# Weights in four pieces and some reordered steps in a recurrent-attention and squared-ReLU kernel

## The chip, the core and the metric

The kernel runs on one core of one Trainium2 chip. The metric is the time of one execution on the device in microseconds (us). The core has five engines that run side by side: PE (TensorE, the matmuls), DVE (VectorE), ACT (ScalarE), POOL (GpSimd) and SP (SyncE, which here only issues transfers). Each engine takes its instructions strictly in the order in which the program lists them; they meet only at semaphores.

## What is computed

The reference first runs a gated recurrence and then a two-layer block on its output:

```
for t in range(S):                                  # B, H, S, D = 4, 8, 768, 48
    state = alpha[:, :, t, :, None] * state + einsum('bhd,bhe->bhde', k[:, :, t], v[:, :, t])
    y[:, :, t] = einsum('bhd,bhde->bhe', q[:, :, t], state)
x = y.transpose(0, 2, 1, 3).reshape(3072, 384)
h = x @ w_in                                        # 384 -> 2048
out = (max(h, 0) ** 2) @ w_out                      # 2048 -> 384
```

Inputs and output are float32; the kernel multiplies in bf16.

## The kernel before, in words

**Units.** The 3072 tokens are cut into 12 units of 256 tokens, numbered 0 to 11 (four batches, three stretches each, all first stretches first). The first unit is unit 0, so the "second unit" of the change is unit 1 and the "third" is unit 2. A unit g passes these steps; the names are those of the kernel's tables, with the line that does the work and the engine:

- `lda`, `ldk`, `ldq`, `ldv` g (L463): load alpha, k, q, v, on SP's queue, or on POOL's for units 1 to 3.
- `pr` (L570, product of two neighbouring decays, DVE or POOL), `ln` (L573, ACT, its logarithm), `m1i` (L579 and L582, PE, running sums into the PSUM bank W), then three readers of that bank on ACT: `ei` (L590), `ea` (L592), `ec` (L595). For units 2 and 3 a second sum `m1s` (L579) goes into the same bank and is read by `es` (L604). For units from 4 on, `lm` (L612, ACT) and `lb` (L614, DVE) take its place.
- `bk`, `aq` (L597 to L608), `eqm0`, `eqm1` (L641), `ekm` (L646): products with decays, all from SBUF to SBUF, on DVE (`bk2` on POOL).
- `tr0`, `tr1` (L669 on PE with copies `et0`, `et1` for units 1 and 2; L657 as transfers on SP from unit 3 on).
- `p` (L877 and L730): scores and state products on PE; `mk0`, `mk1` (L894, DVE) apply the mask; `sa`, `sc`, `sd` carry the state.
- `y` (L757, L765, PE): the unit's output; `xe`, `xf` (L911, L913) copy it out; `xt` (L929, PE, for units 1 to 3) transposes it; `xv` (L941) copies that into the operand of the first layer.
- `s1_g_u`, u from 0 to 7 (L992, PE): a group of six matmuls, the first layer for 256 of the 2048 hidden columns. `re` g_u (L1000 on ACT, L1002 on DVE) is max(h, 0) out of PSUM, `sq` (L1010, L1013, L1014) the square.
- `s2_g_j_s` (L1038, PE): four matmuls each, the second layer; `oe` copies its result out, `out` stores it.

**The order.** Five tables (L206 to L268), one for each engine, write down every instruction's place by name. PE follows its table without overtaking. `+512` and `+256` are matmuls on zeros (L1086) that fill PE's first 17 us.

**The hidden groups' banks.** The first 16 first-layer groups, in the order unit 0 then unit 1, use the PSUM banks that this string names, and all later groups alternate between 0 and 1:

```
HIDDEN = "0102102102102101"
```

The digit 2 is bank O, 0 and 1 are the two H banks. A group that comes into a bank must wait until the `re` of the group that held it before has read it. So group s1_0_5 (the sixth digit) and group s1_1_0 (the ninth) both use H bank 0, s1_0_7 and s1_1_2 use H bank 1, and s1_2_0 and s1_2_2 use H bank 0.

**The weights.** `w_in` and `w_out` are loaded on POOL's queue and converted to bf16 on the way (`weight`, L426 to L436). `PIECES` (L317) says how 16 blocks of 128 hidden columns are cut into transfers: 8, 4 and 4 of them. Inside a piece the columns are dealt out with a stride that is the piece's number of blocks (`hidden`, L417). Group s1_g_u needs blocks 2u and 2u+1, so it waits for one piece. `AFTER` (L1063) holds back transfers until an earlier one has landed: unit 2's alpha (`lda2`) until unit 1's v, each piece of `w_out` likewise, unit 4's alpha until unit 3's.

Of the kernel before, what the change touches and what calls it, by code (L numbers as in the profile page):

```python
# [26 lines left out]
class Program:  # L27
# [12 lines left out]
    def add(self, eng, fn, cost, prio, reads=(), writes=(), name="", dma=None, lag=0, after=(), mode=("F", "F"),  # L40
            alts=None):

        reads, writes = ([h for k in keys for h in ((k + (0,), k + (1,)) if len(k) == self.HALVED.get(k[0]) else (k,))]
                         for keys in (reads, writes))
        choices = {eng: (fn, cost)}
        if alts:
            choices.update(alts)
        op = Op(choices, prio, name)
        op.idx = len(self.ops)
        op.lag = lag  # L50
        op.mode = mode
        if dma is not None:
            if dma not in self.dma_sems:
                self.dma_sems[dma] = self.nc.alloc_semaphore("d_" + dma)
                self.dma_count[dma] = 0
            self.dma_count[dma] += 1
            op.sem = (dma, self.dma_count[dma])
        for o in after:
            op.deps[o] = True
        for k in reads:  # L60
            w = self.writer.get(k)
            if w is not None:
                op.deps[w] = True
            if k[0] == "ps":
                for r in self.readers.get(k, ()):
                    if r not in op.deps:
                        op.deps[r] = False
                        op.shared.add(r)
        for k in writes:
            w = self.writer.get(k)  # L70
            if w is not None:
                op.deps[w] = True
            for r in self.readers.get(k, ()):
                if r is not op:
                    op.deps.setdefault(r, False)
                    op.shared.discard(r)
        for k in reads:
            self.readers.setdefault(k, []).append(op)
        for k in writes:
            self.writer[k] = op  # L80
            self.readers[k] = []
        op.deps.pop(op, None)
        self.ops.append(op)
        return op
# [88 lines left out]
    def emit(self):  # L173
# [33 lines left out]
    "act": """  # L207
        table ln0_0 ln1_0 ei0_0 xcaus ea0_0 ei1_0 ea1_0 ec1_0 et00_0 ec0_0 vc0 ln1 et01_0 et11_0 vc1 ei1 ea1 xe0
        ec1 xv0 sa1 re0_0 re0_1 sq0_1 re0_3 xe1 re0_4 re0_5 ln2 re0_6 sq0_6 ei2 ea2 ec2 vc2 re1_2 es2 re1_3
        re1_4 et0_2 sq1_3 re1_6 sa2 sq1_6 oe0_0 ln3 ei3 ea3 ec3 oe0_1 es3 xf2 xe2 lm4 ln4 vc3 ei4 ea4 ec4 re2_0  # L210
        re2_1 es4 oe1_0 re2_2 re2_3 re2_4 ldk5 re2_5 ldq5 sa3 sq2_5 lm5 re2_7 ln5 re2_6 xe3 ei5 ea5 ec5 xv3 es5
        oe2_0 re3_0 oe2_1 lm6 re3_1 xe4 ln6 re3_4 re3_3 ei6 ea6 ec6 re3_6 sq3_5 re3_7 sq3_7 es6 re4_0 re4_1
        re4_2 re4_3 vc6 xe5 lm7 ln7 re4_7 oe3_1 re4_4 ei7 ea7 ec7 re4_6 sq4_6 es7 oe4_0 re5_0 re5_1 lm8 ln8 xe6
# [7 lines left out]
    "dve": """  # L221
        zero zlinc zlstr zident zcaus zcaus1 zla0 zla1 zones zown zown0 zown1 zqk0 zqk1 zqk2 zlb0 zlb1 ekm0_0
        eqm0_0 ekm1_0 eqm1_0 et10_0 mk0_0 sa0 mk1_0 ekm1 eqm0_1 eqm1_1 et0_1 et1_1 sc0 mk1_1 mk0_1 sc1 re0_2 xf1
        sq0_3 pr2 xv1 sq0_5 re0_7 re1_0 re1_1 ekm2 sq0_7 aq2 eqm0_2 eqm1_2 re1_5 et1_2 sq1_1 sq1_5 re1_7 mk1_2
        pr3 sq1_7 sc2 mk0_2 bk3 eqm1_3 ekm3 aq3 eqm0_3 pr4 xv2 bk4 lb4 ekm4 eqm1_4 eqm0_4 sq2_1 mk1_3 mk0_3 sc3
        oe1_1 sd3 sq2_7 sq2_6 xf3 lb5 ekm5 eqm1_5 eqm0_5 sa4 mk1_4 mk0_4 re3_2 pr6 sc4 sq3_1 xf4 sq3_3 re3_5
        sq3_6 lb6 ekm6 sa5 mk0_5 sc5 mk1_5 eqm0_6 eqm1_6 oe3_0 xf5 sq4_1 re4_5 pr7 sq4_3 sq4_7 sq4_5 bk7 lb7
        eqm0_7 sa6 eqm1_7 ekm7 sc6 sd6 mk0_6 mk1_6 pr8 oe4_1 xf6 sq5_3 bk8 lb8 ekm8 sq5_5 sq5_6 sa7 mk0_7 sc7
# [6 lines left out]
    "pe": """  # L235
        +512 +512 +512 +512 +512 +512 +512 +512 m10_0 m11_0 +512 +512 +256 +256 tr00_0 +512 +256 tr10_0 +512
        +256 +256 tr01_0 p0_0 tr11_0 kv0 +512 +512 +512 +256 +256 p1_0 m11 +512 +256 y0 +512 +512 +256 tr0_1 xt0
        tr1_1 +512 +512 +512 +256 p0_1 s1_0_0 s1_0_1 s1_0_3 s1_0_2 y1 s1_0_4 s1_0_5 xt1 s1_0_6 s1_0_7 m1i2
        s1_1_0 s1_1_1 s1_1_2 m1s2 s1_1_3 s1_1_4 tr0_2 s1_1_6 s1_1_5 tr1_2 s2_0_0_0 s1_1_7 p0_2 s2_0_0_1 s2_0_0_2
        s2_0_0_3 s2_0_1_0 s2_0_1_1 m1i3 s2_0_1_2 s2_0_1_3 m1s3 y2 s2_1_0_0 s2_1_0_1 xt2 s2_1_0_2 m1i4 s1_2_0  # L240
        s1_2_1 s2_1_0_3 s1_2_2 s1_2_3 s2_1_1_0 s1_2_4 s2_1_1_1 s1_2_5 p0_3 s2_1_1_2 s1_2_6 s1_2_7 s2_1_1_3 y3
        m1i5 s2_2_0_0 s2_2_0_1 xt3 s2_2_0_2 s2_2_0_3 s1_3_0 p0_4 s2_2_1_0 s2_2_1_1 s2_2_1_2 s2_2_1_3 s1_3_2
        s1_3_1 y4 s1_3_4 s1_3_3 m1i6 s1_3_6 s1_3_5 s2_3_0_0 s2_3_0_1 s1_3_7 p0_5 s2_3_0_2 s1_4_0 s1_4_1 s2_3_0_3
# [11 lines left out]
        s2_11_0_3 s2_11_1_0 s2_11_1_1  # L255
    """,
    "pool": """
        slinc slstr sident scaus scaus1 ldk1 ldv1 ldq1 win0 win1 win2 lda2 sd0 ldq2 ldv2 ldk2 wout0 sd1 wout1
        wout2 lda3 ldq3 ldk3 ldv3 bk2 sd2 sq2_3 vc4 pr5 bk5 sd4 vc5 bk6 sd5 sq5_1 vc7 sq8_1 vc10
    """,  # L260
    "sp": """
        lda0 ldk0 ldq0 ldv0 lda1 lda4 ldk4 ldq4 ldv4 tr0_3 tr1_3 lda5 tr0_4 out0_1 tr1_4 ldv5 lda6 ldk6 tr1_5
# [8 lines left out]
def pe_ns(count, cols, at_once=1):  # L271
    return count * max(cols / 2.4 + 2.5, 25) / at_once


def act_ns(n):
    return 180 + n * 0.8333
# [10 lines left out]
def bass_gla_recurrent__then__act_relu_squared_kernel(  # L287
# [26 lines left out]
    ACT_LOADS = {5: "kq"}  # L314
    RATIO = 4
    NRAW, NQKS, NKQT, NPM, NV, NXT, NGT, NRR, NOSB = 4, 3, 3, 2, 4, 4, 3, 4, 2
    PIECES = {"win": (0, 8, 12, 16), "wout": (0, 8, 12, 16)}  # L317
    LATE_STATE = (1, 2)
    ROW_TILED = tuple(range(1, G))
    BY_HEADS = (0,)  # L320
# [96 lines left out]
    def hidden(fj):  # L417

        w = piece("win", fj)
        lo, hi = PIECES["win"][w:w + 2]  # L420
        return slice(lo * 128 + fj - lo, hi * 128, hi - lo)

    def piece(key, fj):
        return next(w for w, end in enumerate(PIECES[key][1:]) if fj < end)

    def weight(key, w):  # L426
        lo, hi = PIECES[key][w:w + 2]
        rows = slice(lo * 128, hi * 128)
        if key == "win":
            src, dst = moe_w_in.rearrange("(kk p) n -> p kk n", p=128)[:, :, rows], WIN[:, :, rows]  # L430
        else:
            src = moe_w_out[rows, :].rearrange("(p e) n -> p (e n)", p=128)
            dst = WOUT[:, lo:hi, :].rearrange("p e n -> p (e n)")
        load_op[key, w] = add("pool", lambda e: e.dma_start(dst, src), 930, W_PRIO[key == "wout"] + w, writes=[(key, w)],
                              name=f"{key}{w}", dma=f"{key}{w}", lag={"win": 8200, "wout": 7700}[key] * (hi - lo) / FT,
                              after=[load_op[AFTER[key, w]]] if (key, w) in AFTER else [])  # L436
# [9 lines left out]
    def load(g):  # L446
        b, i = units[g]
        t0 = i * T
        p0 = g * P
        r, la, qs, kt, pm, vb, x2 = (g % n for n in (NRAW, 2, NQKS, NKQT, NPM, NV, 2))  # L450
        first, last = i == 0, i == NST - 1
        sr, sw = 2 * b + i % 2, 2 * b + (i + 1) % 2

        for j, t, nm in ((0, alpha, "a"), (1, k, "k"), (2, q, "q"), (3, v, "v")):
            src = t[b, :, t0:t0 + T, :].rearrange("h (p j) d -> p h (j d)", j=2)
            dst, key = RAW[r][:, j], ("raw", r, j)
            ring, cost, gate = "sp", 600, AFTER.get((g, nm), AFTER.get(g))
            if nm in POOL_LOADS.get(g, ""):
                ring, cost = "pool", 930
            elif nm in ACT_LOADS.get(g, ""):  # L460
                ring, cost = "act", 600
            dst = dst.rearrange("p h j d -> p h (j d)")
            load_op[g, nm] = add(ring, lambda e, dst=dst, src=src: e.dma_start(dst, src), cost, (L_PRIO[g] + j if ring != "pool" else W_PRIO[2] + 10 * g + j),  # L463
                writes=[key], name=f"ld{nm}{g}", dma=f"{nm}{r}{ring}", lag=1230,
                after=([load_op[gate]] if gate else []))
# [479 lines left out]
    def last_tile(gt, rows, p0):  # L945

        for h, cut in enumerate((slice(0, LAST_CUT), slice(LAST_CUT, DM))):
# [3 lines left out]
            def s2(pe, psS=psS, cut=cut):  # L951
# [4 lines left out]
            add("pe", s2, pe_ns(FT, n), p0 + h, reads=[("gt", gt, fj) for fj in range(FT)]  # L956
                + [("wout", w) for w in range(len(PIECES["wout"]) - 1)], writes=[keyS], name=f"s2_{G - 1}_1_{h}")
            add("act", lambda e, psS=psS, cut=cut: e.activation(OSL[:, cut], psS, AF.Copy), act_ns(n), p0 + 700 + h,
# [102 lines left out]
    for g in range(4, G + 2):  # L1061
        ORDER += [f"f{g}"] * (g < G) + [f"y{g - 2}", f"d{g - 2}"]
    AFTER = {(1, "k"): (0, "k"), 2: (1, "v"), ("wout", 0): (1, 'v'),  # L1063
             ("wout", 1): (1, 'v'), ("wout", 2): (1, 'v'), 4: (3, "a")}
    load(0)
    load(1)
    for w in range(len(PIECES["win"]) - 1):
        weight("win", w)
    load(2)
    for w in range(len(PIECES["wout"]) - 1):  # L1070
        weight("wout", w)
# [46 lines left out]
```

## Time and profile before

| | |
|---|---|
| time, median of 3 runs | 171.61 us (171.33 to 172.21) |
| the profiled execution's own time | 171.61 us |
| its span, first to last instruction | 169.9 us |
| PE busy | 165.2 us, 97% of the span |
| DVE, ACT, POOL busy | 119.1, 108.7, 32.1 us |
| bytes moved | 33.37 MB, mean 196 GB/s |

The span lies 1.7 us below the time of the same execution; that rest is outside the instructions. A busy time on PE counts a matmul until its result has left the array, so neighbouring matmuls overlap in the list: a group of six first-layer matmuls is listed with 0.82 us, but the next group starts 0.66 us after it. A timeline row gives the start in us, the duration in us, the engine, the line, the operation, the tile written and the tiles read, and in brackets the idle time of the engine before it with what ended it. In the view of a tile, "DMA to landing" is the time from a transfer's issue until its semaphore is complete.

### The profile page before, as it was taken

The page shows a single profiled execution, that of the slowest core. Times are in us where ns is not written, and L with a number is a line of the kernel's source. Part 1 is how long each engine was busy: PE and PEld are TensorE (multiplying, and loading weights), DVE is VectorE, ACT ScalarE, POOL GpSimd, SP SyncE. Part 2 cuts the span into 40 slices and gives each one's busy share as a digit, 9 for nine tenths or more (in the row PEclk, how much of TensorE's full clock was granted, in tenths as well). Part 3 has the DMA queues.
Part 4 walks back from the last instruction along what each step waited for, and adds up shares of the span by engine and source line. Part 5 has one row for each costly group of instructions (what it writes and reads, how often), then busy time and mean ns, then how long its engine had stood idle before and what let it go on. Part 6 is the DMA issues. An engine that isn't in the chain of part 4 may idle for free.

```text
span 169.9 us, 5395 instructions
## 1 busy us (share of the span) xinstructions
PE 165.2 (97%) x2375; PEld 128.4 (76%) x2375; DVE 119.1 (70%) x207; ACT 108.7 (64%) x210; POOL 32.1 (19%) x42
## 2 busy tenths in 40 slices
PE   7999899999999999999999999999999999999994
PEld 2655899756886797877888877788697788788773
DVE  6477798997859868975978977878969737342130
ACT  3877599658868288667477757474677464466440
POOL 4661895010162032100240000000510000000000
PEclk9999999999999999999999999999999999999999
DMA  5999999999999978999999999999797681050012
GB/s 130 324 317 182 254 317 214 276 307 290 159 222 320 236 187 202 274 155 222 322 200 246 273 118 218 247 220 278 157 187 202 94 118 62 0 145 0 32 61 93
DMA packets 68791, 33.37 MB, mean 196 GB/s; under 512 B 64512, under 2 KB 65536, under 8 KB 68768
## 3 DMA queue, kind: packets, MB, share of 16 engines
q1 hardware_dynamic: 63824, 24.78, 65.7%
q0 software_dynamic: 2864, 7.47, 17.7%
q10 hardware_dynamic: 2080, 0.79, 2.1%
q8 instruction: 18, 0.29, 0.7%
q14 instruction: 5, 0.04, 0.1%
HBM read 25.17 MB, written 4.72 MB: 176 GB/s over the span
## 4 chain that ended last, share of the span: by engine, by line
PE 85%; DMA 8%; DVE 2%; POOL 2%; ACT 1%; issue 0%; SPq 0%
PE psWH L992 36%; PE psO L1038 33%; DMA win<-in_moe_w_in_dram 6%; DMA raw<-in_k_dram 2%; PE psX L877 2%; PE psZ L765 2%; POOL raw L463 2%; PE psX L953 2%; PE psO L992 2%; PE psWH L730 1%; PE psWH L579 1%; PE psZ L877 1%; PE psX L765 1%; PE psWH L1038 1%; DVE qks L641 1%; PE psZ L669 1%
## 5 line engine op out<-in xcount | busy, mean ns | idle before, releaser
L992 PE MATMUL psWH<-xt,win 128*128 128x256 bf16 x552 | 70.6, 273 | 0.5 <-DMA win<-in_moe_w_in_dram 0.5
L1038 PE MATMUL psO<-wout,gt 128*128 128x384 bf16 x352 | 66.7, 326 | 0.0
L992 PEld LDWEIGHTS psWH<-xt,win 128*128 128x128 bf16 x552 | 61.5, 129 | 5.7 <-DMA win<-in_moe_w_in_dram 0.6
L1000 ACT ACTIVATE rr<-psWH 128x512 bf16<-128x512 f32 x79 | 46.8, 598 | 26.7 <-PE psWH L992 25.3
L1038 PEld LDWEIGHTS psO<-wout,gt 128*128 128x128 bf16 x352 | 32.8, 98 | 16.7 <-DVE gt L1010 0.2
L1010 DVE TENSOR_TENSOR gt<-rr 128x1024 bf16<-128x1024 bf16 (+1 forms) x46 | 26.6, 584 | 22.4 <-ACT rr L1000 22.4
L894 DVE TENSOR_TENSOR pm<-psZ,caus 128x1024 bf16<-128x1024 f32 x12 | 14.6, 1218 | 3.6 <-PE psWH L730 3.1
L1013 POOL TENSOR_TENSOR gt<-rr 128x1024 bf16<-128x1024 bf16 x3 | 5.7, 1895 | 56.9 <-ACT rr L1000 56.9
L1045 ACT ACTIVATE osb<-psO 128x384 f32<-128x384 f32 x17 | 8.4, 494 | 11.0 <-PE psO L1038 10.6
L894 DVE TENSOR_TENSOR pm<-psX,caus 128x1024 bf16<-128x1024 f32 x12 | 14.6, 1217 | 0.9 <-PE psX L877 0.5
L641 DVE TENSOR_TENSOR qks<-raw,eq 128x384 bf16<-128x384 f32 x22 | 11.4, 553 | 1.1 <-ACT eq L616 1.0
L646 DVE TENSOR_TENSOR qks<-raw,ek 128x768 bf16<-128x768 f32 x11 | 10.5, 953 | 1.2 <-ACT ek L558 0.8
L1002 DVE TENSOR_SCALAR rr<-psWH 128x512 bf16<-128x512 f32 x13 | 8.9, 688 | 2.3 <-PE psWH L992 2.3
L1086 PE MATMUL psO<-zero 128*128 128x512 bf16 (+1 forms) x31 | 9.0, 421 | 1.3 <-DVE zero L382 1.3
L1014 ACT ACTIVATE gt<-rr 128x512 bf16<-128x512 bf16 (+1 forms) x11 | 9.0, 821 | 0.6 <-DVE rr L1002 0.4
L573 ACT ACTIVATE lab<-prd 128x384 bf16<-128x384 f32 x10 | 5.2, 522 | 5.7 <-DVE prd L570 5.6
L913 DVE CAST xbf<-psZ 128x384 bf16<-128x384 f32 x10 | 5.5, 555 | 3.2 <-PE psZ L757 3.1
L850 POOL TENSOR_TENSOR sbd<-tmp,acm 128x192 bf16<-128x192 f32 x5 | 2.9, 589 | 24.9 <-DVE tmp L840 20.5
L570 DVE TENSOR_TENSOR prd<-raw 128x384 f32<-128x384 f32 x9 | 6.6, 733 | 0.7 <-DMA raw<-in_alpha_dram 0.7
L911 ACT ACTIVATE xbf<-psX 128x384 bf16<-128x384 f32 x11 | 5.4, 488 | 2.0 <-PE psZ L757 1.9
L637 ACT ACTIVATE vbf<-raw 128x768 bf16<-128x768 f32 x7 | 5.9, 843 | 1.1 <-DMA raw<-in_v_dram 1.0
L1086 PEld LDWEIGHTS psO<-zero 128*128 128x128 bf16 x31 | 2.9, 111 | 4.3 <-issue 2.1
(134 smaller groups left out, 191.9 us busy)
## 6 DMA issues: line engine op xcount, KB each, us to landing
out_dram<-osb SPq DMA_DIRECT2D x11, 384.0 KB, 3.5
raw<-in_alpha_dram SPq DMA_DIRECT2D x10, 384.0 KB, 5.0
raw<-in_v_dram SPq DMA_DIRECT2D x9, 384.0 KB, 4.5
raw<-in_k_dram SPq DMA_DIRECT2D x8, 384.0 KB, 6.1
raw<-in_q_dram SPq DMA_DIRECT2D x8, 384.0 KB, 4.4
raw<-in_k_dram POOLq DMA_DIRECT2D x3, 384.0 KB, 6.8
raw<-in_v_dram POOLq DMA_DIRECT2D x3, 384.0 KB, 6.6
raw<-in_q_dram POOLq DMA_DIRECT2D x3, 384.0 KB, 6.5
```

The source lines that it names most:

```text
L570: add("dve", lambda e: e.tensor_tensor(hd(PRD[la][:]), al(0), al(1), ALU.mult), dve_ns(HD), p0, reads=[("raw", r, 0)], writes=[("prd", la) ...
L641: add("dve", lambda e, j=j, dst=dst: e.tensor_tensor(dst, RAW[r][:, 2, :, j, :].rearrange("p (n x) d -> p n x d", x=2), EQ[la][:, j].rearr ...
L646: add("dve", lambda e, a=a, E=E: e.tensor_tensor(QKS[qs][:, a, :, :, 0:D], RAW[r][:, 1 + a].rearrange("p h j d -> p j h d"), E[la][:].rear ...
L894: add("dve", lambda e, hf=hf, psT=psT: e.tensor_tensor(PM[pm][:, hf].rearrange("p r n j t -> p (r n) (j t)"), psT[:, :, :].rearrange("p r ...
L992: ins = pe.matmul(psN[:, i * T:(i + 1) * T], WIN[:, kk, hidden(fj)], mov, start=(kk == 0), stop=(kk == KT - 1))
L1000: add("act", lambda e, psN=psN, rr=rr: e.activation(rr, psN, AF.Relu), act_ns(512), pu + 600, reads=[keyN], writes=[("rr", rb, half)], nam ...
L1002: alts={"dve": (lambda e, psN=psN, rr=rr: e.tensor_scalar(rr, psN, 0.0, None, ALU.max), dve_ns(512))})
L1010: add("dve", lambda e, dst=dst, sq=sq: e.tensor_tensor(dst, sq, sq, ALU.mult), 148 + k * 267, pu + 1200, reads=[("rr", rb, h) for h in ran ...
L1014: "act": (lambda e, dst=dst, sq=sq: e.activation(dst, sq, AF.Square), act_ns(k * 512))})
L1038: ins = pe.matmul(psS, GT[gt][:, fj, j, :], WOUT[:, fj, :], start=(fj == 0), stop=(fj == FT - 1))
L1045: add("act", lambda e, j=j, psS=psS: e.activation(OSB[ob][:, j], psS, AF.Copy), act_ns(DM), ps_ + 700, reads=[keyS], writes=[("osb", ob, j ...
L1086: pr.arrange(TABLES, lambda n: lambda pe: pe.matmul(psO[:, 0:n], ZERO[:, 0:128], ZERO[:, 0:n], skip_group_check=True), zero)
```

## The change

1. Both weights are cut in four equal pieces of four blocks instead of 8, 4 and 4. There is one more transfer of each on POOL's queue (`win3`, `wout3`); the bytes stay.
2. On POOL's queue, unit 2's alpha (`lda2`) goes out behind the third piece of `w_in` and ahead of the fourth.
3. PE: unit 1's transposes `xt1` move one group forward, ahead of s1_0_5; unit 1's first group s1_1_0 moves ahead of s1_0_6 and so right behind s1_0_5; s1_0_7 goes behind `m1i2`. `m1i3` goes back by one second-layer group, `m1i4` goes behind s1_2_0.
4. DVE: `xv1` goes ahead of `pr2`, `re1_0` ahead of `re0_7`. `pr4` leaves DVE and runs on POOL behind `sd2`.
5. ACT: `ln4` goes ahead of `lm4`.

The bank string, the buffers and all arithmetic stay as they are.

```diff
 "act":
-... oe0_1 es3 xf2 xe2 lm4 ln4 vc3 ei4 ea4 ec4 re2_0
+... oe0_1 es3 xf2 xe2 ln4 lm4 vc3 ei4 ea4 ec4 re2_0
 "dve":
-sq0_3 pr2 xv1 sq0_5 re0_7 re1_0 re1_1 ekm2 ... aq3 eqm0_3 pr4 xv2 bk4 lb4
+sq0_3 xv1 pr2 sq0_5 re1_0 re0_7 re1_1 ekm2 ... aq3 eqm0_3 xv2 bk4 lb4
 "pe":
-s1_0_4 s1_0_5 xt1 s1_0_6 s1_0_7 m1i2 s1_1_0 s1_1_1 s1_1_2 m1s2
+s1_0_4 xt1 s1_0_5 s1_1_0 s1_0_6 m1i2 s1_0_7 s1_1_1 s1_1_2 m1s2
-s2_0_1_0 s2_0_1_1 m1i3 s2_0_1_2 s2_0_1_3 m1s3 y2 s2_1_0_0 s2_1_0_1 xt2 s2_1_0_2 m1i4 s1_2_0 s1_2_1 s2_1_0_3 s1_2_2
+s2_0_1_0 s2_0_1_1 s2_0_1_2 m1i3 s2_0_1_3 m1s3 y2 s2_1_0_0 s2_1_0_1 xt2 s2_1_0_2 s1_2_0 m1i4 s1_2_1 s2_1_0_3 s1_2_2
 "pool":
-win0 win1 win2 lda2 sd0 ldq2 ldv2 ldk2 wout0 sd1 wout1 wout2 lda3 ldq3 ldk3 ldv3 bk2 sd2 sq2_3
+win0 win1 win2 lda2 win3 sd0 ldq2 ldv2 ldk2 wout0 sd1 wout1 wout2 wout3 lda3 ldq3 ldk3 ldv3 bk2 sd2 pr4 sq2_3
-PIECES = {"win": (0, 8, 12, 16), "wout": (0, 8, 12, 16)}
+PIECES = {"win": (0, 4, 8, 12, 16), "wout": (0, 4, 8, 12, 16)}
 AFTER gains ("wout", 3): (1, 'v')
```

## The prediction on record

> **What bounds the kernel now.** I read the page's busy times first, then PE's list of waits, then the instructions of PE from 44 us on, grouped by line.
>
> ```profile
> PE 165.2 (97%) x2375; PEld 128.4 (76%) x2375; DVE 119.1 (70%) x207; ACT 108.7 (64%) x210; POOL 32.1 (19%) x42
> PE psO L1086 <- DVE zero L382: 1.3, 1, 1.3
> PE psWH L992 <- DMA win<-in_moe_w_in_dram: 0.5, 1, 0.5
> PE psZ L669 <- DVE qks L646: 0.2, 1, 0.2
> L1038 PE MATMUL psO<-wout,gt 128*128 128x384 bf16 x320 | 60.7, 326 | 0.0
> L992 PE MATMUL psWH<-xt,win 128*128 128x256 bf16 x468 | 59.6, 273 | 0.0
> ```
>
> PE is busy for 97% of the span and has three waits that the profile counts, 2.0 us together. From 44 us on its two big groups (the last rows; the last number is the idle time ahead of them) have no idle time. So the end is PE's list of work plus every gap in it: whatever makes PE wait anywhere after the first weights comes out at the end in full, unless a later gap swallows it. The only gap that the change can aim at is the 0.5 us at `win`. The chain of waits shows the pace of PE's groups:
>
> ```profile
> 27.41 0.66 PE psWH L992 x6
> ...
> 31.14 0.65 PE psO L1038 x4
> ```
>
> A first-layer group (six matmuls) and a second-layer group (four) each take PE 0.65 us. That is 109 ns for 256 columns and 163 ns for 384, so the time goes with the columns streamed, and another stride of the weights changes nothing on PE.
>
> **The transfers.** The view of the tile `win` gives three issues and the time of each to landing, POOL's timeline and the view of `raw` the same for unit 2's alpha:
>
> ```profile
> L434 POOL DMA_DIRECT2D win<-in_moe_w_in_dram x3: 754/757/769, 8.7 to 10.2; - x3
> DMA to landing us min/median/max: 9.7/10.9/12.1
> 12.37 0.93 POOL L463 DMA_DIRECT2D raw<-in_alpha_dram  x1 [1.46 <-DMA raw<-in_v_dram]
> DMA to landing us min/median/max: 11.0/11.0/11.0
> ```
>
> The issues are at 8.7, 9.4 and 10.2 us, so the pieces land at 18.4, 20.3 and 22.3, alpha at 23.4. The half-size pieces follow each other by 2.0 us. In quarters the first 8 blocks land as two pieces, at about 16.4 and 18.4, the third quarter at 20.3 (as before). Alpha then needs its 1.1 us and lands at 21.4, and the last quarter at 23.4. POOL pays another 0.76 us of issue for `win3` at 13.3 (12.37 + 0.93), while it waits for unit 0's state anyway, and at most as much for `wout3`, ahead of `bk2`.
>
> PE's scores of unit 1 are done half a microsecond before the old first piece lands, at 17.9. The first quarter is there by then, so **the wait goes: −0.49** (the list rounds it to 0.5). The second quarter (18.4) is wanted two groups later, at 19.2, the third (20.3) a group ahead of `xt1`, at 21.4, the last (23.4) at about 24.6 by the terms below: no new wait for weights. Alpha, 2 us earlier, is hidden, since `pr2` now stands behind `xv1`, which starts after 22.5.
>
> **Unit 1's first group.** These rows of PE, ACT and DVE give a group's own end, the delay to its reader, the reader's length and the way back to PE:
>
> ```profile
> 20.45 0.82 PE L992 MATMUL psWH<-xt,win 128*128 128x256 bf16 x6
> 21.30 0.69 DVE L1002 TENSOR_SCALAR rr<-psWH 128x512 bf16<-128x512 f32 x1 [0.68 <-PE psWH L992]
> 22.06 0.48 ACT L911 ACTIVATE xbf<-psX 128x384 bf16<-128x384 f32 x1
> 23.17 0.50 PE L929 MATMUL psX<-ident,xbf 128*128 128x128 bf16 x6
> 40.96 0.52 ACT L573 ACTIVATE lab<-prd 128x384 bf16<-128x384 f32 x1 [0.58 <-DVE prd L570]
> 41.54 0.34 PE L579 MATMUL psWH<-lab,linc 128*128 128x384 bf16 x1
> L1000 ACT ACTIVATE rr<-psWH 128x512 bf16<-128x512 f32 x79 | 46.8, 598 | 26.7 <-PE psWH L992 25.3
> ```
>
> A group is complete 0.82 us after it starts, its reader starts 0.03 later (21.27 to 21.30), ACT needs 0.60 for the reading and DVE 0.69, and PE resumes 0.06 after what it waited for (41.48 to 41.54).
>
> Group s1_1_0 uses the same bank as s1_0_5 and now stands directly behind it. In the old order three pieces of work lay between them. Now PE stands still until ACT's `re0_5` is done: 0.82 + 0.03 + 0.60 + 0.06 − 0.66 = **+0.85**. Everything else on PE is queued behind it. ACT is free then, as `re0_4` is long done.
>
> `xt1` a group earlier: the later of its inputs, `xe1`, ended at 22.54; moved up by 0.49 and with 0.06 to PE that is 22.11, while PE is free at 23.17 − 0.66 − 0.49 = 22.02: **+0.09**.
>
> Group s1_1_2 uses the bank of s1_0_7, and s1_0_7 moved back to within one group of it. Its reader `re0_7` is on DVE: 0.82 + 0.03 + 0.69 + 0.06 less the groups s1_0_7 and s1_1_1 (1.31) = **+0.29**.
>
> What follows, `m1i2`, `ei2`, `bk2` on POOL, `ekm2`, slides with PE: `ei2` must let `re0_6` and `sq0_6` pass on ACT, and `bk2` the extra issue on POOL. By my count `ekm2` ends at 29.2, just when PE comes to `tr0_2`. The old order met there too:
>
> ```profile
> 26.55 1.05 POOL L597 TENSOR_TENSOR ek<-ek,raw 128x384 f32<-128x384 f32 x1
> 27.64 0.96 DVE L646 TENSOR_TENSOR qks<-raw,ek 128x768 bf16<-128x768 f32 x1 [0.31 <-POOL ek L597]
> 28.65 0.62 PE L669 MATMUL psZ<-ident,qks 128*128 128x128 bf16 x8
> ```
>
> `ekm2` ended at 28.60 and `tr0_2` started at 28.65, so PE had waited a little for it. For that and for the slow first group behind the old wait for weights I credit 0.14, an estimate. At `tr0_2` the sum is −0.49 + 0.85 + 0.09 + 0.29 − 0.14 = **+0.60**.
>
> **The sums of unit 3.** `m1s3` writes the bank that `ei3`, `ea3`, `ec3` read. The old order put two second-layer groups between `m1i3` and `m1s3`, the new one puts one:
>
> ```profile
> 36.54 0.32 PE L579 MATMUL psWH<-lab,linc 128*128 128x384 bf16 x1
> 36.80 1.46 PE L1038 MATMUL psWH<-wout,gt 128*128 128x384 bf16 x8
> 38.10 0.33 PE L579 MATMUL psWH<-lab,lstr 128*128 128x384 bf16 x1
> 36.98 0.49 ACT L590 ACTIVATE ek<-psWH 128x384 f32<-128x384 f32 x1 [0.63 <-PE psWH L582]
> 37.73 0.18 ACT L595 ACTIVATE acm<-psWH 128x8 f32<-128x8 f32 x1
> ```
>
> `ec3` ends 1.37 after `m1i3` starts, with the 0.06 that is 1.43. PE's work in between is 0.26 + 0.65. **+0.52**, with `m1s3`, `y2` and all after it queued behind. It would hide only if ACT got shorter.
>
> **`pr4` on POOL, s1_2_0 ahead of `m1i4`.** Rows of SP, PE, DVE and POOL:
>
> ```profile
> L463 SPq DMA_DIRECT2D raw<-in_alpha_dram x1: 368/368/368, 35.2 to 35.2; - x1
> DMA to landing us min/median/max: 4.5/4.5/4.5
> 40.64 0.81 PE L1038 MATMUL psO<-wout,gt 128*128 128x384 bf16 x4
> 40.37 0.55 DVE L570 TENSOR_TENSOR prd<-raw 128x384 f32<-128x384 f32 x1
> 40.84 0.56 DVE L941 COPY xt<-psX 128x768 bf16<-128x768 bf16 x1
> 48.95 1.00 POOL L572 TENSOR_TENSOR prd<-raw 128x384 f32<-128x384 f32 x1 [0.29 <-DMA raw<-in_alpha_dram]
> 83.71 1.90 POOL L1013 TENSOR_TENSOR gt<-rr 128x1024 bf16<-128x1024 bf16 x1 [13.94 <-ACT rr L1000]
> 85.07 0.94 DVE L570 TENSOR_TENSOR prd<-raw 128x384 f32<-128x384 f32 x1
> ```
>
> In the old order PE was free at 41.29 (40.64 + 0.65) and waited for `m1i4` until 41.54: 0.25. Now it waits for `xv2` instead. `xt2` gives it up 0.5 after its start, `xv2` takes 0.56, and one group covers part: about 0.16. That is −0.09. Against it: unit 4's alpha lands at 39.7 (35.2 + 4.5), so POOL starts the product right among `bk3`, `eqm1_3`, `ekm3`, `aq3`, `eqm0_3` on DVE. These began behind `ei3` (36.98 + 0.49) and ended where `pr4` begins, at 40.4; with the 0.60 and the one group by which `m1i3` is later they run from 38.7 to 41.7. At 85.07 such a product on DVE took 0.94 instead of the 0.55 at 40.37, beside a POOL instruction that ended at 85.61: the two held each other up. If POOL's 1.00 us goes between DVE's in full, less the 0.2 of start-up that overlaps, `eqm0_3` ends at 42.5, `xv2` at 43.0, and PE waits 0.6: +0.37. Ends −0.09 and +0.37; who asks first at 39.7 no row shows, so I take the middle, **+0.15**. By the Trainium skill ("SBUF — State Buffer", section "Who interferes with whom") a DVE instruction with two SBUF inputs and a GpSimd one that reads SBUF exclude each other for the whole instruction; by that my upper end would hold, and the sum would be 173.4.
>
> **s1_2_2** shares its bank with s1_2_0, and `re2_0` stands behind `ei4`, `ea4`, `ec4` on ACT:
>
> ```profile
> 42.12 0.47 ACT L590 ACTIVATE ek<-psWH 128x384 f32<-128x384 f32 x1
> 42.92 1.10 ACT L1000 ACTIVATE rr<-psWH 128x512 bf16<-128x512 f32 x2
> ```
>
> From `m1i4`: 0.44 to `ei4` (as at 36.54 and 36.98), 0.80 more to `re2_0`, 0.60, 0.06: 1.90. PE has only `m1i4`, s1_2_1 and s2_1_0_3 meanwhile, 1.58, since s1_2_0 went ahead: **+0.32**. The swap of `ln4` and `lm4` costs nothing, as both are done by 42.5.
>
> **The sum**: 0.60 + 0.52 + 0.15 + 0.32 = +1.59 us. The profiled execution's own time is 171.61, which is also the median shown, so **173.2 us**, +0.9%. Bounds of the unsure terms (`tr0_2` up to 0.4 late, POOL and DVE −0.24 to +0.22) give 172.8 to 173.8 for this case.
>
> **The rivals.**
> - *Half of it* (0.20): the waits up to `tr0_2` hold, but the two around unit 3 and 4 are hidden, because `m1s3` and s1_2_2 find their readers earlier than rows that slid with PE suggest. For it: ACT has idle time there (0.63 before `ei3`). Against: that idle time is its wait for PE. 171.61 + 0.60 = 172.2.
> - *Not slower* (0.17): the delay is swallowed between 44 and 160 us. It decides from a total of 1.6 us of gaps there that hang on transfers and not on PE's own progress. For it: the chain of waits has steps there that do not join, as below. Against: PE's idle times read 0.0, and what releases PE there, ACT and DVE, will be as late as PE is. 171.6.
>
> ```profile
> 61.57 1.43 PE psWH L992 x12
> 63.24 1.34 PE psWH L992 x12
> ```
>
> - *The gain alone* (0.10): the readers come in time, and the 0.49, the 0.25 at `m1i4` and 0.14 fall away with nothing in their place: 170.7. Against it stand the shared banks.
> - *The change does not bring the weights in time* (0.06): each extra transfer costs one of the 2.0 us steps. Then the last quarter lands at 25.4, s1_0_6 waits 0.9 more: 174.1. For it speaks only that the whole load waits on one queue; against it, that 384 KB pieces already follow at the pace of the 768 KB one. The Trainium skill ("DMA: Bandwidth & Descriptors", section "Anatomy of one DMA — SWDGE (gpsimd) path") gives each such transfer about 2.0 us of fixed time; if these did not overlap, this rival would hold. The rows have pieces 2.0 us apart in all, so they overlap.
>
> **How the numbers follow.** Forecast 0.47, rivals 0.20, 0.17, 0.10, 0.06. A measurement of this kernel can tell about 0.5% (0.86 us) from no change. Slower by more than that are the forecast, the late weights and a little of the half case: 0.57. Faster by more is the gain alone, whose 170.7 lies at that bound: 0.10. The rest, 0.33, is within. Leaving out the gain alone and the late weights, the range is 171.4 to 174.0.
>
> **What would show it.** In the changed kernel PE should start the first layer at 17.9 with no wait for `win`; a hole of 0.85 us ahead of s1_1_0 near 23.9; one of 0.3 ahead of s1_1_2; `m1s3` 1.43 after `m1i3`; the wait ahead of s1_2_2; and the old list of PE from there on, some 1.6 us late. It is wrong if these holes are missing, or if they are there and PE is back on the old times by 100 us.

## The result, and the profile after

| | before | changed |
|---|---|---|
| median, 6 runs each | 171.64 us (171.33 to 172.21) | 173.28 us (172.94 to 175.85) |
| ratio, 95% interval | | 1.0115 (1.0078 to 1.0152) |
| the profiled execution: time, span | 171.61, 169.9 us | 172.94, 171.2 us |

The change made the kernel 1.6 us slower by the medians and 1.33 us by the two profiled executions. The forecast was 173.2. The ratios here and below leave out executions more than 1.5% above the fastest of their kernel (here the one of 175.85 us), so they are not the quotients of the medians. First PE's list of waits in the changed kernel (us in total, times, longest):

```profile
PE psWH L992 <- ACT rr L1000: 1.0, 2, 0.8
PE psWH L992 <- DVE xt L941: 0.4, 1, 0.4
PE psWH L579 <- ACT acm L595: 0.4, 1, 0.4
```

The wait for `win` is gone, and three new kinds have come, each at a reader of a PSUM bank or of a copy out of one. PE's timeline has their places:

```profile
17.43 1.50 PE L992 MATMUL psWH<-xt,win 128*128 128x256 bf16 x12
...
21.99 0.82 PE L992 MATMUL psWH<-xt,win 128*128 128x256 bf16 x6
23.59 0.82 PE L992 MATMUL psWH<-xt,win 128*128 128x256 bf16 x6 [0.78 <-ACT rr L1000]
...
25.84 0.82 PE L992 MATMUL psO<-xt,win 128*128 128x256 bf16 x6
26.78 0.85 PE L992 MATMUL psWH<-xt,win 128*128 128x256 bf16 x6
...
28.94 0.61 PE L669 MATMUL psZ<-ident,qks 128*128 128x128 bf16 x8
...
37.34 0.33 PE L579 MATMUL psWH<-lab,linc 128*128 128x384 bf16 x1
...
37.60 0.81 PE L1038 MATMUL psWH<-wout,gt 128*128 128x384 bf16 x4
38.77 0.34 PE L579 MATMUL psWH<-lab,lstr 128*128 128x384 bf16 x1 [0.36 <-ACT acm L595]
...
41.33 0.81 PE L1038 MATMUL psO<-wout,gt 128*128 128x384 bf16 x4
42.58 0.84 PE L992 MATMUL psWH<-xt,win 128*128 128x256 bf16 x6 [0.44 <-DVE xt L941]
...
44.20 0.81 PE L1038 MATMUL psO<-wout,gt 128*128 128x384 bf16 x4
45.19 1.06 PE L992 MATMUL psWH<-xt,win 128*128 128x256 bf16 x8 [0.19 <-ACT rr L1000]
```

A group of six, or a second-layer group, keeps PE for 0.65 to 0.66 us, so the hole ahead of s1_1_0 is 23.59 − 21.99 − 0.66 = 0.94 us. The others are 0.28 ahead of s1_1_2 (26.78), 0.52 ahead of `m1s3` (38.77), 0.59 ahead of s1_2_0 (42.58) and 0.33 ahead of s1_2_2 (45.19). The idle time in brackets is smaller, since a matmul counts as busy until it has left the array.

The step that the reader should look at twice is `tr0_2` at 28.94: in the kernel before it stood at 28.65. Holes of 1.41 us lie ahead of it (0.94, 0.28 and another 0.19 ahead of `xt1`), and yet it is only 0.29 us late. The earlier start makes up nearly all of the difference: the first group stands at 17.43 instead of 18.42, that is 0.99 us earlier and not the forecast 0.49. The other half us is not the wait for `win`, since unit 1's scores ended that much earlier. They follow the landing of unit 1's v. POOL's issue of `lda2` waits for the same landing and so marks it, here at 11.90 instead of 12.37:

```profile
11.90 0.93 POOL L463 DMA_DIRECT2D raw<-in_alpha_dram  x1 [1.07 <-DMA raw<-in_v_dram]
```

In each of the profiles of this document that has no wait for `win`, the first group starts 5.5 to 5.6 us behind that issue (17.43 − 11.90 = 5.53).

At `tr0_2` itself PE did not wait in the changed kernel: `ekm2` ended at 27.87 + 0.96 = 28.83, and PE came 0.11 us later. These are `bk2` and `ekm2`:

```profile
26.83 1.01 POOL L597 TENSOR_TENSOR ek<-ek,raw 128x384 f32<-128x384 f32 x1
27.87 0.96 DVE L646 TENSOR_TENSOR qks<-raw,ek 128x768 bf16<-128x768 f32 x1 [0.49 <-POOL ek L597]
```

So PE's own list, holes included, set `tr0_2` here, with another chain close behind it. The experiments show what that chain is worth.

The transfers came early enough (the view of `win` for its four pieces):

```profile
L434 POOL DMA_DIRECT2D win<-in_moe_w_in_dram x4: 747/762/782, 8.6 to 12.8; - x4
DMA to landing us min/median/max: 6.8/8.3/9.8
```

The first piece lands at 15.4 (forecast 16.4), the last (issued at 12.8) at 22.6, and s1_0_6 starts at 24.25.

### The profile page after: what moved, and what is told of

Same layout as the page of the kernel before. It is cut to its first block, busy times and chain, and to the rows that moved or that the text cites. A ratio compares the mean times of both kernels' runs of the same rounds, so it can differ in the third digit from the quotient of the medians.

```text
span 171.2 us, 5397 instructions
## 1 busy us (share of the span) xinstructions
PE 165.0 (96%) x2373; PEld 126.4 (74%) x2375; DVE 119.3 (70%) x206; ACT 108.3 (63%) x210; POOL 34.8 (20%) x45
## 3 DMA queue, kind: packets, MB, share of 16 engines
q0 software_dynamic: 3408, 7.47, 17.9%
## 4 chain that ended last, share of the span: by engine, by line
PE 90%; DVE 5%; ACT 2%; issue 1%
PE psWH L992 36%; PE psO L1038 33%; PE psO L1086 3%; PE psX L877 3%; PE psZ L765 2%; PE psZ L877 2%; PE psX L953 2%; PE psWH L730 1%; PE psZ L669 1%; PE psX L765 1%; PE psWH L579 1%; PE psO L992 1%; PE psWH L1038 1%; DVE qks L515 1%; DVE eq L608 1%
## 5 line engine op out<-in xcount | busy, mean ns | idle before, releaser
L992 PEld LDWEIGHTS psWH<-xt,win 128*128 128x128 bf16 x552 | 59.4, 114 | 8.6 <-ACT rr L1000 1.0
L1010 DVE TENSOR_TENSOR gt<-rr 128x1024 bf16<-128x1024 bf16 (+1 forms) x46 | 26.6, 584 | 22.7 <-ACT rr L1000 22.6
L1086 PE MATMUL psO<-zero 128*128 128x512 bf16 (+1 forms) x29 | 8.2, 411 | 1.6 <-DVE zero L382 1.2
L590 ACT ACTIVATE ek<-psWH 128x384 f32<-128x384 f32 x10 | 4.9, 491 | 2.2 <-PE psWH L582 2.2
L599 DVE TENSOR_TENSOR ek<-ek,raw 128x384 f32<-128x384 f32 x7 | 3.9, 555 | 3.0 <-ACT ek L590 3.0
```

Source lines behind the costliest of these rows:

```text
L992: ins = pe.matmul(psN[:, i * T:(i + 1) * T], WIN[:, kk, hidden(fj)], mov, start=(kk == 0), stop=(kk == KT - 1))
L1010: add("dve", lambda e, dst=dst, sq=sq: e.tensor_tensor(dst, sq, sq, ALU.mult), 148 + k * 267, pu + 1200, reads=[("rr", rb, h) for h in ran ...
L1086: pr.arrange(TABLES, lambda n: lambda pe: pe.matmul(psO[:, 0:n], ZERO[:, 0:128], ZERO[:, 0:n], skip_group_check=True), zero)
```

## The experiments

My theory at first: each hole is PE waiting for a reader, and the holes add up, less 0.5 us for the wait that is gone. The rival: the additional transfers and their issue time cost the time. After the first four runs (quarters alone, the bank string, `m1i3`, unit 4) the theory had to be amended, and the next four tell the amended one from the first. Each ratio is against the kernel before, timed beside the run on the same chip.

**Quarters alone.**

```diff
-PIECES = {"win": (0, 8, 12, 16), "wout": (0, 8, 12, 16)}
+PIECES = {"win": (0, 4, 8, 12, 16), "wout": (0, 4, 8, 12, 16)}
-win0 win1 win2 lda2 ... wout2 lda3          (POOL)
+win0 win1 win2 win3 lda2 ... wout2 wout3 lda3
```

> Weights in quarters alone, every other step in the old order (the fourth quarter of w_in ahead of the third unit's alpha). Waits theory: only the old wait for the first piece goes, so 0.5 us faster than the kernel before (ratio 0.997), PE's first-layer work starting 0.5 us earlier with no wait for win. Transfer theory (the two more transfers and their issue time are what costs): slower than before by 0.5 to 1.5 us, with PE waiting for win or with unit 2's products late.

Measured: 171.57 us, ratio 1.0004 (0.9987 to 1.002). Neither theory as a whole: there is no gain and no loss. PE's timeline:

```profile
17.33 1.50 PE L992 MATMUL psWH<-xt,win 128*128 128x256 bf16 x12
...
28.63 0.62 PE L669 MATMUL psZ<-ident,qks 128*128 128x128 bf16 x8 [0.64 <-DVE qks L646]
```

PE starts the first layer 1.1 us before the old time, and `tr0_2` stands at 28.63, where it stood. The wait has moved there: `tr0_2` needs `ekm2`, and that needs `bk2` on POOL. POOL's timelines, first the kernel before, then this one:

```profile
17.71 0.50 POOL L850 TENSOR_TENSOR sbd<-tmp,acm 128x192 bf16<-128x192 f32 x1 [4.41 <-DVE tmp L843]
26.55 1.05 POOL L597 TENSOR_TENSOR ek<-ek,raw 128x384 f32<-128x384 f32 x1
```

```profile
17.17 0.51 POOL L850 TENSOR_TENSOR sbd<-tmp,acm 128x192 bf16<-128x192 f32 x1 [4.52 <-DVE tmp L843]
21.31 1.68 POOL L434 DMA_DIRECT2D wout<-in_moe_w_out_dram  x3
26.50 1.08 POOL L597 TENSOR_TENSOR ek<-ek,raw 128x384 f32<-128x384 f32 x1
```

From `sd0` to `bk2` POOL is busy without a pause, mostly with issuing transfers: 8.84 us before, 9.33 with one more issue for `wout3` (three in 1.68 us). In this execution v landed 0.62 us earlier than before (`lda2` goes out at 11.75), so that `sd0` too starts 0.54 us earlier, and POOL's list, 0.49 us longer, eats that.

**The kernel before once more**, for a second profile. No edit.

> The kernel before once more, for a second profile. If the 0.5 us by which the changed kernel's scores of unit 1 ended earlier (17.4 instead of 17.9) is a difference between executions, set by when unit 1's v lands (11.5 to 12.2 us in the ten profiles so far), this profile can have either; if quarters bring it, 17.9 again. Time 171.6.

171.80 us, its profiled execution 171.74. Here the first piece landed at 17.4 (8.6 + 8.8), and PE did not wait for it:

```profile
17.86 1.53 PE L992 MATMUL psWH<-xt,win 128*128 128x256 bf16 x12
...
28.64 0.62 PE L669 MATMUL psZ<-ident,qks 128*128 128x128 bf16 x8 [0.20 <-DVE qks L646]
```

The wait of 0.49 us that the change aimed at is absent in this execution, and `tr0_2` is at 28.64 again, the time the same. **The wait was worth nothing in the kernel before**: without it PE waits at `tr0_2`. In both profiles of that kernel `lda2` goes out at 12.37 and unit 1's scores end at 17.9. Of the twelve profiles with w_in in quarters, ten have `lda2` at 11.75 to 12.13 and two (the bank string, `pr4` on DVE) at 12.46. So what moves the start is the landing of v; whether quarters bring an earlier landing, so few profiles can't settle.

**Another bank string**, order and transfers as changed.

```diff
-HIDDEN = "0102102102102101"
+HIDDEN = "0102101022102101"
```

> The changed kernel with another bank string: s1_0_6 gets H bank 1, s1_0_7 H bank 0, s1_1_0 bank O, so no group stands right behind one of its own bank; order and transfers as changed. Waits theory: the hole of 0.94 us ahead of s1_1_0 and the one of 0.29 ahead of s1_1_2 go; what is left ahead of s1_1_0 is its operand xv1 (some 0.1), so about 1.1 us less than the changed kernel, some 172.1 us, ratio 1.003. Rival (the order itself is late, by ACT and the transfers): no gain, as s1_0_6 then waits for the last quarter or tr0_2 for ekm2.

173.25 us, ratio 1.0076 (1.0051 to 1.0101).

```profile
17.95 1.50 PE L992 MATMUL psWH<-xt,win 128*128 128x256 bf16 x12
...
22.52 0.82 PE L992 MATMUL psWH<-xt,win 128*128 128x256 bf16 x6
23.33 0.85 PE L992 MATMUL psO<-xt,win 128*128 128x256 bf16 x6
...
29.27 0.62 PE L669 MATMUL psZ<-ident,qks 128*128 128x128 bf16 x8 [0.61 <-DVE qks L646]
```

The holes at the shared bank are gone (0.15 left ahead of s1_1_0, none ahead of s1_1_2), so they came from the bank. But `tr0_2` stands 11.32 us behind the first group; in the changed kernel that was 28.94 − 17.43 = 11.51. Removing 1.1 us of holes brought 0.2, because PE now waits for `ekm2`, as the last clause of the rival had it: `bk2` starts 27.16 − 17.79 = 9.37 us behind `sd0`, in the changed kernel 26.83 − 17.27 = 9.56. The expectation of 172.1 fell.

**`m1i3` at its old place.**

```diff
-s2_0_1_2 m1i3 s2_0_1_3          (PE)
+m1i3 s2_0_1_2 s2_0_1_3
```

> The changed kernel with m1i3 back at its old place, two second-layer groups ahead of m1s3. Waits theory: the hole of 0.52 us ahead of m1s3 goes, 0.5 us less than the changed kernel (172.8, ratio 1.0085). Rival (that wait only moves): PE waits the same time at m1i3 for ln3 or at s1_2_0 for xv2, and the time stays at 173.3.

174.51 us, ratio 1.0109 (1.006 to 1.0159), no gain in the median. In the trace the hole ahead of `m1s3` is gone (38.29 follows 36.99 + 1.30), and s1_2_2 stands 27.11 us behind the first group instead of 27.76. In the profiled execution (174.13 us) the gain was lost further on:

```profile
58.56 0.42 PE L877 MATMUL psX<-kqt 64*64 64x128 bf16 x16 [1.73 <-issue]
```

That is `p0_4`. It needs unit 4's second transpose, `tr1_4`, whose issue and landing SP's view of `kqt` gives:

```profile
L657 SPq DMA_TRANSPOSE kqt<-qks x1: 2738/2738/2738, 48.4 to 48.4; - x1
DMA to landing us min/median/max: 10.1/10.1/10.1
```

48.4 + 10.1 = 58.5. So the word "issue" stands for a transfer here. In all six profiles with such a wait, `p0_4` starts within 0.2 us after this landing. In the kernel before the transpose landed after 6.4 us, at 54.8, with 1.1 us to spare; in the changed kernel's profile after 7.9, at 57.2, with `p0_4` at 57.37.

**Unit 4's steps as before**: `pr4` on DVE, `lm4 ln4`, `m1i4 s1_2_0`.

```diff
-sd2 pr4 sq2_3 (POOL);  eqm0_3 xv2 (DVE);  ln4 lm4 (ACT);  s1_2_0 m1i4 (PE)
+sd2 sq2_3     (POOL);  eqm0_3 pr4 xv2;    lm4 ln4;        m1i4 s1_2_0
```

> The changed kernel with unit 4's steps as before: pr4 on DVE, lm4 ahead of ln4, m1i4 ahead of s1_2_0. Waits theory: the hole ahead of s1_2_0 shrinks from 0.60 to the old 0.25 us and the 0.33 ahead of s1_2_2 goes, 0.68 us less than the changed kernel (172.6, ratio 1.0076). Rival (these holes are swallowed later anyway): within 0.2 us of the changed kernel.

172.43 us, ratio 1.006 (1.0035 to 1.0085): 0.85 us below the changed kernel, with 0.68 expected. In the trace s1_2_2 stands 0.61 us nearer to the first group (44.59 − 17.44 = 27.15). The profiled execution is one of the long ones, 174.26 us, with 1.89 us of wait ahead of `p0_4` (`tr1_4` landed at 48.2 + 10.4 = 58.6).

**All three undone at once** (bank string, `m1i3`, unit 4).

> The changed kernel with all three undone at once: the other bank string, m1i3 at its old place, unit 4's steps as before. Theory after the first four runs (POOL's list of transfer issues, one longer, sets when bk2, ekm2 and so tr0_2 come, and hides most of the two early holes): 0.2 + 0.5 + 0.7 us less than the changed kernel, 171.9 us, ratio 1.001. Rival (the recorded sum, each hole in full): 1.2 + 0.5 + 0.7 us less, 170.9 us, ratio 0.996.

171.77 us, ratio 1.0016 (0.9998 to 1.0034). The amended theory's 171.9 holds, the rival's way of adding (170.9) does not: the wait is again at `tr0_2`, 0.62 us of it. The profiled execution is the longest of its twelve, 172.97 us, with 1.26 us of wait ahead of `p0_4`, although unit 4's steps stand at their old times here.

The fastest executions, which a late transpose should touch least, go down in the same steps: 172.94 us for the changed kernel, 172.68 with the other bank string, 172.34 with `m1i3` moved back, 172.08 with unit 4's steps as before, 171.44 with all three. With 6 or 12 executions each this is a hint and not a test.

**`pr4` on DVE, `m1i4` left where the change put it.**

```diff
-aq3 eqm0_3 xv2 (DVE);  sd2 pr4 (POOL);  ln4 lm4 (ACT)
+aq3 eqm0_3 pr4 xv2;    sd2;             lm4 ln4
```

> The changed kernel with pr4 back on DVE ahead of xv2 (and lm4 ahead of ln4), m1i4 still behind s1_2_0. If POOL's pr4 and DVE's aq3 held each other up (1.47 and 1.35 us instead of 1.00 and 0.55), aq3 is back at 0.55 us, the hole ahead of s1_2_0 falls from 0.60 to 0.3 although pr4 now stands ahead of xv2, and the kernel is 0.3 us faster than the changed one. Rival (aq3 was late for es3): aq3 stays long and the hole at 0.6 or more.

The trace agrees: the hole ahead of s1_2_0 is 0.27 us, and `aq3` is back at its old length. DVE and POOL in the changed kernel, then DVE here:

```profile
40.11 1.35 DVE L608 TENSOR_TENSOR eq<-eq,raw 128x384 f32<-128x384 f32 x1
```

```profile
39.58 1.47 POOL L572 TENSOR_TENSOR prd<-raw 128x384 f32<-128x384 f32 x1 [2.81 <-DMA raw<-in_alpha_dram]
```

```profile
40.69 0.55 DVE L608 TENSOR_TENSOR eq<-eq,raw 128x384 f32<-128x384 f32 x1
```

The time does not show the 0.3 us: 173.84, ratio 1.0114 (1.0086 to 1.0142). This profile too has a wait ahead of `p0_4`, 1.29 us.

**One issue less on POOL**: the run with the other bank string, and w_out in three transfers, of which the first fills two quarters.

> The kernel with the other bank string, and w_out in the old three transfers (the first of them fills both quarters), so one issue of 0.57 us less on POOL ahead of bk2. POOL theory: bk2, ekm2 and tr0_2 come 0.5 us earlier counted from the end of unit 1's scores (10.8 instead of 11.3), 0.5 us less than the run with the bank string alone, about 172.7 us. Rival (ekm2 is late for ACT's ei2): no change.

`tr0_2` stands 10.96 us behind the first group instead of 11.32; 0.36 of the expected 0.5 (the issue of the double piece took 0.72 us instead of 0.58). The time, 173.14 (ratio 1.0093, 1.006 to 1.0127), says nothing here, as the profiled execution loses 1.5 us at `p0_4`.

**`bk2` ahead of `ldv3` on POOL**, `w_in` in quarters, `w_out` in three transfers, all other orders old.

> Weights of w_in in quarters, w_out in the old three transfers, all orders old except that bk2 goes ahead of ldv3 on POOL. POOL theory: ekm2 comes up to 1 us earlier than with the quarters alone, the hole of 0.64 us ahead of tr0_2 goes, and the early start is kept: 0.5 to 0.8 us faster than the kernel before, 170.9 us, ratio 0.996. Rival (something else holds the pace from there): no faster than before.

`tr0_2` came at 27.77 (10.16 behind the first group), with no wait. The next one follows:

```profile
30.72 0.81 PE L1038 MATMUL psO<-wout,gt 128*128 128x384 bf16 x4 [0.56 <-DMA wout<-in_moe_w_out_dram]
```

The first piece of `w_out`, again of double size, was late. 171.51 us, ratio 1.0016 (0.9983 to 1.0048): no faster than before, as the rival had it.

**The changed kernel once more, and with `tr1_4` ahead of the store on SP.**

```diff
-tr0_4 out0_1 tr1_4 ldv5          (SP)
+tr0_4 tr1_4 out0_1 ldv5
```

> The changed kernel once more, beside the next one: 173.3 us, single executions up to 176, those with a wait of 1 to 2 us ahead of p0_4 near 57 us.

> The changed kernel with unit 4's second transpose tr1_4 ahead of the store out0_1 on SP's queue. If the executions of 174 to 176 us come from p0_4 waiting for that transpose (it landed 7.3 to 10.4 us after its issue in the profiles with w_in and w_out in quarters, the wait appearing from about 8), it is issued 0.9 us earlier, the wait ahead of p0_4 is gone or 0.9 us shorter and the median falls to about 172.9. Rival (the instruction stream of PE itself is late there, as the profile's word issue would have it): no change in the spread.

174.01 us (173.03 to 175.70) and 173.15 us (173.03 to 173.98). The changed kernel has thus given 173.28 and 174.01 without any edit, so medians of six of these kernels can't tell 0.5 us apart; above, the traces do. The first one's profile has 0.65 us of wait ahead of `p0_4` (57.59 to 58.24; `tr1_4` landed at 49.1 + 9.0 = 58.1), the second none, with the landing at 48.6 + 7.4 = 56.0:

```profile
57.44 0.42 PE L877 MATMUL psX<-kqt 64*64 64x128 bf16 x16
```

So the long executions are, in the profiles that caught one (up to 174.55 us), those in which this transpose lands late; none of 175 us or more has a profile. Six runs each do not make more of it than that.

**A version meant to beat both**: both weights in quarters, all orders old but for `bk2` ahead of `ldv3` and `tr1_4` ahead of `out0_1`.

> A version meant to beat both: both weights in quarters, all orders of PE, DVE and ACT old, bk2 ahead of ldv3 on POOL, tr1_4 ahead of out0_1 on SP. POOL theory: no hole ahead of tr0_2, and with w_out in quarters no wait for its first piece either (0.56 in the run with bk2 early and the old pieces): the 0.5 us of the early start stays, 171.0 us, ratio 0.9965. Rival: PE's gain is lost again at the next reader.

171.50 us, ratio 0.9992 (0.9973 to 1.0011), the profiled execution 171.11 us. `tr0_2` is at 27.77 and w_out is not waited for; of that 0.9 us, `m1i4` has 0.49 left (41.05 against 41.54), after 0.3 lost at `m1i3` to a reader on DVE. It is not shown to be faster than the kernel before.

## Why the prediction was right, and where it was not

The sign, the places and the mechanism hold: every term of the sum is found on PE in the changed kernel. That the time came within 0.1 us is in part luck, since single terms missed in both directions and unit 1's v landed earlier than the sum assumed.

- **The wait that goes, −0.49: right on PE, but worth nothing alone.** The first group starts 5.53 us behind the issue of `lda2` instead of 6.05, so 0.52 are gone. Alone they bring nothing, as the second profile of the kernel before shows: PE then waits at `tr0_2` for POOL's list. In the changed kernel they count only because the holes push PE past that list. The text had seen that `ekm2` and PE meet at `tr0_2` with nothing to spare, but not said that the gain hangs on the holes.
- **s1_1_0 behind its bank, +0.85; `xt1`, +0.09; s1_1_2, +0.29.** The holes measure 0.94, 0.19 (`xt1` at 21.66 behind 20.81 + 0.66) and 0.28. In the first, `re0_5` ended at 23.45 and PE resumed 0.14 us later, where the text had 0.06. The bank string takes the first and last away, but without them `tr0_2` comes only 0.2 us earlier, as POOL's list is the next limit.
- **The sum at `tr0_2`**, +0.60 on record, was +0.29 (28.94 against 28.65): −0.99 for the start, +1.41 for the holes, −0.13 for small losses of the old order (0.14 were credited). The record lacks the 0.50 us by which unit 1's scores ended earlier, and 0.18 us of the holes.
- **`m1s3`, +0.52: right**, 0.52 by the trace, gone when `m1i3` moves back. It delays `m1s3` by 0.38 us more than `tr0_2` (38.77 against 38.10), because the old order had lost 0.13 in between, ahead of `tr1_2` and `m1i3`.
- **`pr4` and s1_2_0, +0.15: mis-sized.** The hole is 0.59 instead of the old 0.25, +0.34, close to the upper end (+0.37). POOL's product and DVE's `aq3` held each other up, which the run with `pr4` on DVE undoes. The trace agrees with the rule cited from the Trainium skill ("SBUF — State Buffer", section "Who interferes with whom").
- **s1_2_2, +0.32: right**, 0.33.
- **The sum at s1_2_2**, +1.59 on record, was 45.19 − 43.81 = +1.38, and +1.33 at the end of the profiled execution; in the changed kernel's second profile it was 45.34 − 43.81 = +1.53. PE gave back almost nothing of it between 45 us and the end. Measured from the issue of `lda2` it was 33.29 − 31.44 = +1.85, in the second profile +1.82. So the steps cost PE some 0.25 us more than forecast, and the landing of v, 0.3 to 0.5 us earlier, hid that.
- **Not foreseen**: a late landing of unit 4's second transpose, which makes PE wait 0.65 to 1.89 us at `p0_4` in six of the profiles. That this is the rest of the median's 1.6 and most of its spread is argued and not shown. It does not come from PE asking earlier: from the issue of `tr1_4` to the place of `p0_4` it is 57.37 − 49.27 = 8.1 us in the changed kernel, 55.96 − 48.41 = 7.55 in the kernel before. The landing takes longer: 7.3 to 10.4 us in the nine profiles of the changed kernel and of the runs made from it, 5.7 to 6.5 in the five of the kernel before and of the runs made from that. Even with all three undone it took 8.6. Why is open.

The rivals: late weights did not come about. The Trainium skill's fixed 2.0 us ("DMA: Bandwidth & Descriptors", section "Anatomy of one DMA — SWDGE (gpsimd) path") was not paid for each in turn: the first two quarters, issued at 8.6 and 9.3, landed 1.6 us apart (8.6 + 6.8 = 15.4 and 9.3 + 7.7 = 17.0), and that with 384 KB each moved in between. The half case fell at `m1s3` and s1_2_2, and the rival without a slowdown fell too, as PE did not catch up by the end. The gain alone fell at the banks. One bound on record does not follow from its terms: 173.2 − 0.24 gives 173.0 and not 172.8.

## What to carry to other kernels

A wait that the profile shows is worth only what the next meeting point leaves of it: before crediting one, follow the other engine's chain to the place where the two meet, and count its issues too, since an additional transfer there lengthens that chain (here by 0.49 us). Before comparing the times of two profiles, look for an input that landed at another time, here unit 1's v, and measure from it. Before moving a matmul, look up which PSUM bank it writes and who must have read that bank; two groups of one bank side by side cost more than the reader's 0.60 us here, 0.94. And when a hole is removed without a gain in time, look for the next wait in the trace before giving up the explanation.

## What the runs showed of the hardware that was not expected

- The two-input product on POOL beside DVE's products from SBUF to SBUF took 1.47 us in the changed kernel's first profile, 1.08 in its second, and 1.29 and 1.79 in the runs with w_out in three and with `tr1_4` ahead, against 1.00 at 48.95 in the kernel before. DVE paid in turn: `aq3` 1.35 instead of 0.55 in the first and the last of these, `ekm3` 1.76 instead of 0.95 in the second. The rows read as turns: in the first profile `ekm3` ran from 39.25 to 40.20, POOL's product then ended at 41.05 and `aq3` at 41.46.
- The same transpose, `tr1_4`, took from 5.7 us (the version meant to beat both) to 10.4 us (unit 4's steps as before) to land. The orders differ a little between these kernels; but even one kernel, the changed one, gave 7.9 and 9.0. What sets it stays open.
- The same piece of weights, in the same kernel, landed at 18.4 in one execution and at 17.4 in another.
